# Attention, GLU and routed experts on one core: side work handed out twice per pair, squares moved to VectorE, the first experts' table a chunk earlier

## The chip, the cores and the metric

The kernel runs on one core of a Trainium2 chip. The metric is the device time of one execution in microseconds (us), taken over several runs. The engines are TensorE (PE; its weight loads are listed as PEld), VectorE (DVE), ScalarE (ACT), GpSimd (POOL) and SyncE (SP, which only issues DMAs here). Each engine works through its own instructions in the order in which they were written and stops at the first one whose inputs are not there.

## The reference, cut to what matters

```python
attn = np.maximum(z @ z.T / S, 0.0) ** 2            # 8 batches, S = 3072, z has 64 columns
x = u * (attn @ v)                                  # 24576 tokens of 256
xn = x / np.sqrt(np.mean(x * x, -1) + 1e-6) * rms_g
g = xn @ w_gate                                     # 256 -> 1536
x = (g * sigmoid(g) * (xn @ w_val)) @ w_out         # 1536 -> 256
e_idx = np.argmax(x @ r_gate, 1)                    # one of 8 experts for each token
for e in range(8):
    ye = np.maximum(x[e_idx == e] @ w1[e], 0.0) @ w2[e]      # 256 -> 1024 -> 256
    out[e_idx == e] = softmax_weight * sigmoid(x @ r_og)[e] * ye
```

Every product is made in float32 accuracy from pairs of a high and a low part, so most of them are three matmuls (high by high, high by low, low by high).

## The kernel before, in words

**Chunks and pairs.** The 24576 tokens are 48 chunks of 512 (six to a batch). For attention a chunk has 12 steps, one for each 256 keys (`Attn`, step n is chunk n // 12); for the GLU it has 12 steps, one for each 128 of the 1536 columns (`Glu`, step m). `pair(n, m)` writes one attention step and one GLU step side by side, with m = n - 18: first 18 attention steps stand alone, then come 558 pairs, then 6 GLU steps alone, and the 12 GLU steps of the last chunk. After these the experts run: 100 slots of 256 gathered tokens, four steps each (`Expert`).

**One pair on the engines.** TensorE gets the scores `s` of step n (L504, L505), the GLU products `g` of step m (L648), then the second halves of the steps before: attention times values into `o` (L535 to L537, `Attn.second`), and the GLU's output `y` (L673 to L675). ScalarE makes relu and square of the scores in `r` (L507, L512) and their high part `ha` (L515), the sigmoid `sg` (L652) and the high part `hg` (L660). VectorE makes the low parts `la` (L521) and `lg` (L663) and multiplies the gate (L656). The scores' tile `r` has two buffers, and four PSUM banks (`sc`) are shared by `s`, `g` and the small products of the side work.

**Side work.** All that a chunk needs between its attention and its GLU, and between its GLU and the experts, is cut into pieces that the class `Side` holds in two streams and a list of loaded jobs. Once in each pair, behind `a.high(0)`, `side.tick` hands out pieces until the pair's budget (4.0 for a pair, 1.5 for attention alone, 1.9 for the GLU alone, all in estimated us) is spent; stream 0 goes first. A piece that is only a time (no function) holds its stream until so much of the planned time has passed (7.94 for a pair, 3.75 and 4.19 for a step alone). `side.after(k, fn)` runs a function k ticks later. `side.until(...)` writes pieces out at once, without regard to a budget, until a condition holds.

**From attention to GLU.** When the last step of a chunk's attention is done, `Attn.leave` multiplies by `u` into `x` (L546, VectorE) and puts into stream 0: a time of 1.0, the squares (L552, four ACTIVATEs with a sum on ScalarE), 3.0, the root (L558 to L564, VectorE and GpSimd), 6.0, the scaling of `x` (L568, ScalarE), 2.0, and 16 block transposes into `xf` (L599 through `turn_x`, VectorE, named `turn_blocks` in the code). This chunk's GLU starts six pairs after its attention has ended. In the last pair ahead of it `until(g.J + 1 in turned)` writes what is left of the transposes, and `split_x` makes `xTh` (L628, ScalarE) and `xTl` (L629, VectorE), which the first `g` of the chunk reads.

**Weights at the start.** The GLU's weights come as 36 blocks of doubles and are decoded by `from_double`: two instructions on VectorE (L333, L334) and a square on ScalarE (L331), then `lower` (three on VectorE, L338 to L340, one on GpSimd, L341), then `parts` (high part on ScalarE, L93, low part on GpSimd, L96). `lower` comes one tick after the first part and `parts` two ticks after that. Two scratch buffers alternate; a decode that finds its buffer's previous decode unfinished writes the rest of that one out first (`chain.end()`). A GLU step m of the first chunk needs 3 (m + 1) decoded blocks and calls `until` for them.

**Experts.** `route` (stream 1) turns a finished chunk of `y` into expert numbers, gates and rows in DRAM (`xs`, `idl`), with 16 block transposes into `rec` (L615). `table(0)` (stream 1) makes the list of the first 12 slots (NSA) from the chunks that are routed by then: it counts, gathers list entries, transposes them on TensorE (`ids`, L894) and keeps them. It is started after GLU step m = 46 * 12, and behind step 3 of the last chunk's GLU `until(0 in tabs)` writes out what is left of it; then `begin_experts` loads weights and rows of slots 0 and 1 and starts the row transposes of slot 0 (`turn_rows`, L599 into `gTf`, which takes one of the two buffers of `sg`).

Of the kernel before, what the change touches and what calls it, by code (L numbers as in the profile page):

```python
# [19 lines left out]
LAG = 3  # L20
# [5 lines left out]
def attention_glu_routed(ctx: ExitStack, tc: tile.TileContext, u, v, z, w_gate, w_val, w_out, rms_g, r_gate, r_og, w1, w2, out):  # L26
# [31 lines left out]
    NSA = max(0, min(12, -((E * 255 - (NT - 1024)) // 256)))  # L58
# [429 lines left out]
    class Attn:  # L488
# [50 lines left out]
        def leave(self):  # L539
# [10 lines left out]
            def squares(k):  # L550
                for qb in (2 * k, 2 * k + 1):
                    nc.scalar.activation(out=uu[:, qb], in_=x[:, qb], func=AF.Square, accum_out=ss[:, qb : qb + 1])  # L552
                if k:
                    squared.add(J)
# [15 lines left out]
            side.add(1.0, None, 0)  # L570
            side.add(0.1, lambda: squares(0), 0)
            side.add(0.1, lambda: squares(1), 0)
            side.add(3.0, None, 0)
            side.add(0.4, root, 0)
            side.add(6.0, None, 0)
            side.add(0.1, lambda: scale(0), 0)
            side.add(0.1, lambda: scale(1), 0)
            side.add(2.0, None, 0)
# [363 lines left out]
    def known(stage):  # L942

        return NT if stage else (NJ - 2) * 512
# [114 lines left out]
    def begin_experts():  # L1059
        for s in range(2):  # L1060
            prepare(s)
            for part in range(4):
                load_weights(s, part)
        turn_rows(0)

    def spare(n):
        side.jobs(ej[:n])
        del ej[:n]
# [5 lines left out]
    last = {"a": None, "g": None}  # L1074
    lists = {}

    def pair(n, m):
# [11 lines left out]
        pa, pg = last["a"], last["g"]  # L1089
        last["a"], last["g"] = a, g  # L1090
        for step in (pa, pg):
            if step:
                step.second()
# [3 lines left out]
        t.time = (3.75 if a else 0.0) + (4.19 if g else 0.0)  # L1097
        t.budget = 4.0 if a and g else 1.5 if a else 1.9
# [15 lines left out]
        if pa and pa.kp == NP - 1:  # L1114
            pa.leave()
        if pg and pg.f == NF - 1 and pg.J < NJ - 1:
            pg.leave()
        if a:
# [13 lines left out]
            if a.J >= 2 and a.kp in (NP // 2, NP - 1):  # L1132
                spare(1)

    with tc.manual_schedule():
# [7 lines left out]
        for n in range(tail + AHEAD):  # L1143
            m = n - AHEAD
            if m == 0:
                side.until(lambda: 0 in turned, 0)
                split_x(0)
            pair(n if n < NJ * NP else None, m if m >= 0 else None)
            if m == (NJ - 2) * NF and NSA:

                table(0, lambda: s1)
# [7 lines left out]
        for f in range(NF):  # L1159
            pair(None, tail + f)  # L1160
            if f == LAG and NSA:
                side.until(lambda: 0 in tabs, 1)
                begin_experts()
# [68 lines left out]
```

## Time and profile before

| what | value |
|---|---|
| median of 3 runs | 6101.07 us (6096.69 to 6106.18) |
| profiled execution, its own time | 6110.35 us |
| its span, first to last instruction | 6108.6 us |
| PE, PEld, DVE, ACT, POOL busy | 96%, 84%, 68%, 56%, 19% |
| mean granted TensorE clock | 0.983 |
| matmuls | 35032 |

The span has these stretches: attention alone from 5.7 us (the first scores) to 124.3 us, pairs from there to 4766.6 us, the last six pairs and the GLU alone to 4928.6 us (the first expert matmul), experts to 6092 us. A row with a window says how long each engine was busy in it and how many instructions it ran; PEclk is the mean of the granted clock, where 1.00 is 2.4 GHz and 0.50 is 1.2 GHz.

### The profile page before, as it was taken

The page shows a single profiled execution, that of the slowest core. Times are in us where ns is not written, and L with a number is a line of the kernel's source. Part 1 is how long each engine was busy: PE and PEld are TensorE (multiplying, and loading weights), DVE is VectorE, ACT ScalarE, POOL GpSimd, SP SyncE. Part 2 cuts the span into 40 slices and gives each one's busy share as a digit, 9 for nine tenths or more (in the row PEclk, how much of TensorE's full clock was granted, in tenths as well). Part 3 has the DMA queues.
Part 4 walks back from the last instruction along what each step waited for, and adds up shares of the span by engine and source line. Part 5 has one row for each costly group of instructions (what it writes and reads, how often), then busy time and mean ns, then how long its engine had stood idle before and what let it go on. Part 6 is the DMA issues. An engine that isn't in the chain of part 4 may idle for free. (4 is left out here: it accounts for less than half of the span.)

```text
span 6108.6 us, 95345 instructions
## 1 busy us (share of the span) xinstructions
PE 5868.4 (96%) x35032; PEld 5155.5 (84%) x35032; DVE 4141.2 (68%) x8920; ACT 3418.4 (56%) x6610; POOL 1151.3 (19%) x1729
## 2 busy tenths in 40 slices
PE   6899999999999999999999999999999889999998
PEld 5688888888888888888888888888888779999998
DVE  6666666665666566666666666657565678888886
ACT  4566666666666666666666666666666423333332
POOL 2212101210121012101211030103000023333333
PEclk8999999999999999999999999999999999999999
DMA  2101100110010001001110010001000112232241
GB/s 70 47 25 49 34 25 30 46 34 23 30 49 30 23 30 49 30 27 32 47 32 22 29 32 13 15 12 36 8 15 8 47 55 101 101 103 101 102 139 57
DMA packets 199592, 268.27 MB, mean 44 GB/s; under 512 B 46988, under 2 KB 176016, under 8 KB 190928
## 3 DMA queue, kind: packets, MB, share of 16 engines
q1 hardware_dynamic: 173664, 210.29, 10.7%
q0 software_dynamic: 25456, 51.83, 2.7%
q8 instruction: 278, 4.55, 0.3%
q14 instruction: 194, 1.59, 0.1%
HBM read 528.71 MB, written 86.71 MB: 101 GB/s over the span
## 5 line engine op out<-in xcount | busy, mean ns | idle before, releaser
L537 PE MATMUL o<-v,la 128*128 128x256 f32 x4608 | 1298.3, 282 | 29.3 <-DVE la L521 29.2
L535 PE MATMUL o<-v,ha 128*128 128x256 f32 x4608 | 1291.9, 280 | 5.3 <-DVE ha L517 5.2
L536 PE MATMUL o<-v,ha 128*128 128x256 f32 x4608 | 1291.2, 280 | 0.0
L521 DVE TENSOR_TENSOR la<-r,ha 128x512 fp32r<-128x512 f32 x1152 | 835.9, 726 | 663.5 <-ACT ha L515 658.0
L507 ACT ACTIVATE r<-s 128x512 f32<-128x512 f32 x1152 | 624.8, 593 | 859.4 <-PE s L505 806.5
L648 PE MATMUL g<-xTh,wg 128*128 128x512 f32 x2304 | 844.7, 408 | 131.9 <-ACT xTh L628 102.7
L656 DVE TENSOR_TENSOR sg<-g,sg 128x512 f32<-128x512 f32 x1152 | 793.9, 689 | 196.0 <-ACT sg L652 133.5
L537 PEld LDWEIGHTS o<-v,la 128*128 128x128 f32 x4608 | 871.5, 189 | 33.2 <-DVE la L521 32.9
L535 PEld LDWEIGHTS o<-v,ha 128*128 128x128 f32 x4608 | 872.6, 189 | 29.5 <-DVE ha L517 6.4
L536 PEld LDWEIGHTS o<-v,ha 128*128 128x128 f32 x4608 | 871.9, 189 | 25.6
L648 PE MATMUL g<-xTh,wv 128*128 128x512 f32 x2304 | 831.2, 402 | 5.7 <-ACT wv L93 3.0
L515 ACT ACTIVATE ha<-r 128x512 fp32r<-128x512 f32 x1116 | 705.7, 632 | 38.6
L512 ACT ACTIVATE r<-r 128x512 f32<-128x512 f32 x1152 | 721.7, 627 | 1.0
L648 PEld LDWEIGHTS g<-xTh,wg 128*128 128x128 f32 x2304 | 443.2, 192 | 263.7 <-ACT xTh L628 122.9
L1007 PE MATMUL h<-gh,W 128*128 128x256 f32 x3200 | 641.2, 283 | 5.4 <-ACT gh L93 4.1
L660 ACT ACTIVATE hg<-sg 128x512 fp32r<-128x512 f32 x576 | 363.6, 631 | 487.2 <-DVE sg L656 431.3
L1026 PE MATMUL eo<-W,hx 128*128 128x512 f32 x1600 | 580.2, 395 | 0.7 <-DVE o L1039 0.7
L1007 PEld LDWEIGHTS h<-gh,W 128*128 128x128 f32 x3200 | 526.9, 191 | 25.3 <-ACT gh L93 5.5
L648 PEld LDWEIGHTS g<-xTh,wv 128*128 128x128 f32 x2304 | 446.1, 194 | 109.9 <-PE g L648 3.8
L599 DVE STREAM_TRANSPOSE gTf<-xg 32x128 f32<-32x128 f32 x1600 | 483.3, 302 | 49.2 <-DMA xg<-xs,clip 26.9
L1010 ACT ACTIVATE hx<-h 128x512 fp32r<-128x512 f32 x400 | 236.7, 595 | 496.0 <-PE h L1007 493.5
L96 POOL TENSOR_TENSOR le<-e_raw,he 128x512 fp32r<-128x512 f32 x64 | 83.0, 1297 | 2119.9 <-ACT he L93 2119.9
(170 smaller groups left out, 11046.8 us busy)
## 6 DMA issues: line engine op xcount, KB each, us to landing
W<-ws SPq DMA_DIRECT2D x400, 1024.0 KB
v_raw<-in_v SPq DMA_DIRECT2D x96, 256.0 KB
u<-in_u SPq DMA_DIRECT2D x48, 512.0 KB
xs<-rec SPq DMA_DIRECT2D x48, 512.0 KB
e_raw<-in_moe_w SPq DMA_DIRECT2D x64, 256.0 KB
ws<-he SPq DMA_DIRECT2D x64, 256.0 KB
ws<-le SPq DMA_DIRECT2D x64, 256.0 KB
z_raw<-in_z SPq DMA_DIRECT2D x48, 128.0 KB
```

The lines of the kernel that those rows point to most:

```text
L507: nc.scalar.activation(out=r, in_=ps, func=AF.Relu, scale=SCALE)
L512: nc.scalar.activation(out=r, in_=r, func=AF.Square)
L515: nc.scalar.activation(out=self.ab[j][0], in_=r, func=AF.Copy)
L521: nc.vector.tensor_tensor(out=l, in0=self.r[j], in1=h.bitcast(F32), op=ALU.subtract)
L535: nc.tensor.matmul(o, lhsT=ah[:, cs], rhs=vh, start=kb == 0 and qb % 2 == 0, stop=False, skip_group_check=True)
L536: nc.tensor.matmul(o, lhsT=ah[:, cs], rhs=vl, start=False, stop=False, skip_group_check=True)
L537: nc.tensor.matmul(o, lhsT=al[:, cs], rhs=vh, start=False, stop=kb == NK - 1, skip_group_check=True)
L599: nc.vector.transpose(out=ov[32 * q : 32 * q + 32, :, :, i, :], in_=iv[32 * i : 32 * i + 32, :, :, q, :])
L648: nc.tensor.matmul(ps, lhsT=a[:, d, fs], rhs=x[:, d], start=n == 0, stop=n == 5)
L656: nc.vector.tensor_tensor(out=self.sg, in0=ps, in1=self.sg, op=ALU.mult)
L1007: nc.tensor.matmul(o, lhsT=w[:, c0 : c0 + 128], rhs=x[:, d], start=n == 0, stop=n == 5)
L1026: nc.tensor.matmul(self.accs[t], lhsT=h[:, cs], rhs=w, start=f == 0, stop=False)
```

## The change

Five things are changed.

- `pair` calls `side.tick` twice, at the old place and at its end, each time with half of the time and half of the budget. `after(k)` therefore counts half pairs, and times such as 3.0 pass within one half pair (3.97).
- In stream 0 the squares come first, right behind the product with `u`, as four `scalar_tensor_tensor` with a sum on VectorE; the root follows at once, and the times are 3.0 and 1.0 where they were 1.0, 3.0, 6.0 and 2.0.
- While attention runs alone, `Attn.second` is written two steps late where it was one; the first pair with a GLU step writes two of them.
- `table(0)` starts after m = 45 * 12 and knows 45 chunks (NSA stays 12), `begin_experts` comes behind step 1 of the last chunk's GLU where it was step 3, and a time of 8.0 stands ahead of the row transposes of slot 0.
- `Attn.leave` is called for each step written.

```diff
-                    nc.scalar.activation(out=uu[:, qb], in_=x[:, qb], func=AF.Square, accum_out=ss[:, qb : qb + 1])
+                    nc.vector.scalar_tensor_tensor(
+                        out=uu[:, qb], in0=x[:, qb], scalar=1.0, in1=x[:, qb], op0=ALU.mult, op1=ALU.mult, accum_out=ss[:, qb : qb + 1]
+                    )
...
-            side.add(1.0, None, 0)
-            side.add(0.1, lambda: squares(0), 0)
-            side.add(0.1, lambda: squares(1), 0)
+            side.add(0.9, lambda: squares(0), 0)
+            side.add(0.9, lambda: squares(1), 0)
+            side.add(0.4, root, 0)
             side.add(3.0, None, 0)
-            side.add(0.4, root, 0)
-            side.add(6.0, None, 0)
             side.add(0.1, lambda: scale(0), 0)
             side.add(0.1, lambda: scale(1), 0)
-            side.add(2.0, None, 0)
+            side.add(1.0, None, 0)
             turn_x(J)
...
-        return NT if stage else (NJ - 2) * 512
+        return NT if stage else (NJ - 3) * 512
...
                 load_weights(s, part)
+        side.add(8.0, None, 0)
         turn_rows(0)
...
-        pa, pg = last["a"], last["g"]
-        last["a"], last["g"] = a, g
-        for step in (pa, pg):
+        pg, last["g"] = last["g"], g
+        if a:
+            last["a"].append(a)
+
+        gone = []
+        while len(last["a"]) > (1 if g and a else 2 if a else 0):
+            gone.append(last["a"].pop(0))
+        for step in (*gone, pg):
             if step:
                 step.second()
...
-        t.time = (3.75 if a else 0.0) + (4.19 if g else 0.0)
-        t.budget = 4.0 if a and g else 1.5 if a else 1.9
+
+        t.time = ((3.75 if a else 0.0) + (4.19 if g else 0.0)) / 2
+        t.budget = 2.0 if a and g else 0.75 if a else 0.95
         side.tick(t)
...
+        side.tick(t)
...
-            if m == (NJ - 2) * NF and NSA:
+            if m == (NJ - 3) * NF and NSA:
...
-            if f == LAG and NSA:
+            if f == 1 and NSA:
```

Where the instructions now stand is shown at three places.

**VectorE ahead of a chunk's GLU** (here chunk 27; `xf` holds the transposed chunk, `xTl` is the low part that `split_x` makes, `la`, `sg` and `lg` belong to the steps of the pairs). Before:

```order
L599 STREAM_TRANSPOSE xf<-x 32x4x2x32 x12
L521 TENSOR_TENSOR la<-r,ha 128x512
L656 TENSOR_TENSOR sg<-g,sg 128x512 x2
L599 STREAM_TRANSPOSE xf<-x 32x4x2x32 x4
L629 SCALAR_TENSOR_TENSOR xTl<-xf,g_p,xTh 128x512 x2
L521 TENSOR_TENSOR la<-r,ha 128x512
L663 TENSOR_TENSOR lg<-sg,hg 128x512
```

After:

```order
L599 STREAM_TRANSPOSE xf<-x 32x4x2x32
L521 TENSOR_TENSOR la<-r,ha 128x512
L656 TENSOR_TENSOR sg<-g,sg 128x512 x2
L521 TENSOR_TENSOR la<-r,ha 128x512
L663 TENSOR_TENSOR lg<-sg,hg 128x512
L521 TENSOR_TENSOR la<-r,ha 128x512
L656 TENSOR_TENSOR sg<-g,sg 128x512 x2
L629 SCALAR_TENSOR_TENSOR xTl<-xf,g_p,xTh 128x512 x2
L521 TENSOR_TENSOR la<-r,ha 128x512
```

Before, all 16 transposes stand in the pair of the split, four of them between the gate's product and `xTl`; now the last of them stands a whole pair earlier, and the others (6 and 9 in a row) in the two pairs before that.

**VectorE in the first chunk's GLU, ahead of the matmuls of its step 9** (`d` is the scratch of a weight decode, `w_raw` the block of doubles, `ss` and `yi` belong to a root). Before:

```order
L663 TENSOR_TENSOR lg<-sg,hg 128x512
L338 SCALAR_TENSOR_TENSOR d<-d 128x256
L339 TENSOR_SCALAR d<-d 128x256
L340 SCALAR_TENSOR_TENSOR d<-w_raw,d 128x256
L338 SCALAR_TENSOR_TENSOR d<-d 128x256
L339 TENSOR_SCALAR d<-d 128x256
L340 SCALAR_TENSOR_TENSOR d<-w_raw,d 128x256
L558 TENSOR_SCALAR ss<-ss 128x4
L559 TENSOR_SCALAR yi<-ss 128x4
```

After, the last two of three decodes that stand there one behind the other:

```order
L333 TENSOR_SCALAR d<-w_raw 128x256
L334 SCALAR_TENSOR_TENSOR d<-w_raw,d 128x256
L338 SCALAR_TENSOR_TENSOR d<-d 128x256
L339 TENSOR_SCALAR d<-d 128x256
L340 SCALAR_TENSOR_TENSOR d<-w_raw,d 128x256
L333 TENSOR_SCALAR d<-w_raw 128x256
L334 SCALAR_TENSOR_TENSOR d<-w_raw,d 128x256
L338 SCALAR_TENSOR_TENSOR d<-d 128x256
L339 TENSOR_SCALAR d<-d 128x256
L340 SCALAR_TENSOR_TENSOR d<-w_raw,d 128x256
L599 STREAM_TRANSPOSE xf<-x 32x4x2x32 x5
```

Before, two decodes were begun earlier and only their second parts stood here; now three whole decodes do, written out by `until` because stream 0 holds the ticks of these pairs.

**TensorE around the transposes of the first table** (`ids`; `y` and `g` are the GLU, `s` the scores). Before:

```order
L674 MATMUL y<-lg,wo_98 128x512
L675 MATMUL y<-hg,wo_99 128x512
L894 MATMUL ids<-ident,plain 128x12 x4
L648 MATMUL g<-xTh,wg_94 128x512
L648 MATMUL g<-xTl,wg_94 128x512
L648 MATMUL g<-xTh,wg_95 128x512
```

After:

```order
L674 MATMUL y<-lg,wo_98 128x512
L675 MATMUL y<-hg,wo_99 128x512
L894 MATMUL ids<-ident,plain 128x12 x4
L504 MATMUL s<-p 128x512
L505 MATMUL s<-q,p 128x512
L504 MATMUL s<-p 128x512
L505 MATMUL s<-q,p 128x512
L648 MATMUL g<-xTh,wg_94 128x512
```

They move from the GLU alone (its step 4 follows) into a pair that still has attention, six pairs ahead of the end of attention.

## Rows read from the trace of the kernel before

**Rows 1.** Windows: us, then busy us (instructions) of PE, PEld, DVE, ACT, POOL; PEclk, DMA share, GB/s.

```profile
5.70:124.30 118.60, 83.53 (x489) 74.57 (x490) 79.72 (x160) 54.13 (x113) 38.20 (x55) 0.88 0.24 71
124.30:144.60 20.30, 9.17 (x42) 7.21 (x41) 15.49 (x35) 9.13 (x19) 2.89 (x4) 0.66 0.09 26
144.60:220.70 76.10, 61.42 (x325) 51.35 (x324) 53.97 (x112) 43.62 (x88) 22.57 (x31) 0.93 0.20 60
220.70:273.50 52.80, 38.40 (x186) 31.38 (x185) 40.77 (x86) 28.32 (x64) 17.00 (x32) 0.87 0.16 50
369.90:4766.60 4396.70, 4295.78 (x24770) 3725.84 (x24769) 2828.51 (x5587) 2808.46 (x5382) 628.35 (x1146) 0.99 0.10 29
4766.60:4928.60 162.00, 135.72 (x643) 111.06 (x642) 96.68 (x223) 60.96 (x117) 13.73 (x25) 0.92 0.16 61
4928.60:5060.00 131.40, 114.68 (x750) 102.81 (x749) 115.95 (x347) 33.33 (x70) 43.36 (x43) 0.95 0.14 42
5060.00:6092.00 1032.00, 1031.81 (x7276) 966.69 (x7275) 846.60 (x2248) 314.24 (x635) 369.88 (x358) 1.00 0.30 103
```

**Rows 2.** Waits of PE from 369.9 to 4766.6: us in total, times, longest.

```profile
PE g L648 <- ACT xTh L628: 79.4, 44, 3.5
PE g L648 <- DVE xTl L629: 11.3, 40, 0.3
```

**Rows 3.** Windows inside the pairs: one chunk of 12, and windows of 50 us.

```profile
2776.00:2873.70 97.70, 96.25 (x562) 83.88 (x561) 63.33 (x125) 63.33 (x121) 10.11 (x19) 1.00 0.09 28
350.00:400.00 50.00, 47.62 (x271) 41.29 (x270) 31.62 (x54) 31.62 (x58) 6.14 (x14) 0.97 0.14 43
550.00:600.00 50.00, 46.10 (x253) 38.94 (x253) 31.95 (x54) 31.92 (x60) 21.72 (x41) 0.93 0.25 77
```

**Rows 4.** Timeline at a chunk's start: start, us, engine, line, tiles, count, [idle before <-releaser].

```profile
2865.78 5.37 DVE L599 STREAM_TRANSPOSE xf<-x 32x256 f32<-32x256 f32 x12
...
2871.79 1.48 DVE L656 TENSOR_TENSOR sg<-g,sg 128x512 f32<-128x512 f32 x2
...
2873.28 1.79 DVE L599 STREAM_TRANSPOSE xf<-x 32x256 f32<-32x256 f32 x4
...
2875.17 1.34 ACT L628 ACTIVATE xTh<-xf,g_p 128x512 fp32r<-128x512 f32 x2 [5.93 <-DVE xf L599]
...
2875.94 0.49 PE L648 MATMUL g<-xTh,wg 128*128 128x512 f32 x1 [1.16 <-ACT xTh L628]
```

**Rows 5.** Groups by shape: busy us, mean ns, idle before.

```profile
L552 ACT ACTIVATE u<-x 128x256 f32<-128x256 f32 x192 | 76.9, 402 | 0.0
L552 ACT ACTIVATION_READ_ACCUMULATOR u<-x 128x1 f32 x192 | 35.9, 187 | 0.0
L338 DVE SCALAR_TENSOR_TENSOR d<-d 128x256 f32<-128x256 f32 x36 | 15.1, 419 | 0.0
L341 POOL TENSOR_TENSOR d<-d 128x256 f32<-128x256 f32 x36 | 27.4, 761 | 132.9 <-DVE d L340 131.4 <-DVE ss L558 1.5
```

**Rows 6.** Waits at the end of the pairs and in the first experts, 4766.6 to 5060, of PE.

```profile
PE g L648 <- ACT xTh L628: 12.2, 2, 11.0
PE ids L894 <- DVE plain L888: 9.3, 1, 9.3
PE eo L1027 <- DVE lx L1013: 7.8, 5, 3.3
PE y L673 <- ACT hg L660: 4.4, 1, 4.4
```

**Rows 7.** Timeline ahead of the last chunk's GLU.

```profile
4847.94 7.17 DVE L599 STREAM_TRANSPOSE xf<-x 32x256 f32<-32x256 f32 x16
```

**Rows 8.** Waits of all engines from 0 to 320.

```profile
PE o L537 <- DVE la L521: 29.2, 15, 4.8
...
PE g L648 <- DVE sg L656: 25.6, 10, 6.8
...
DVE d L333 <- POOL wv L96: 13.5, 7, 3.4
...
DVE d L333 <- POOL wo L96: 11.8, 6, 2.9
DVE d L333 <- POOL wg L96: 11.6, 7, 2.2
...
PE g L648 <- ACT xTh L628: 11.1, 1, 11.1
```

## What the prediction says

> **What bounds the kernel now.** I read the windows first, to see in which stretch TensorE is idle or slow; then who it waits for there; then the timeline of one such wait; and last the groups by shape, for prices.
>
> [rows 1] split the span. From 5060 on TensorE is busy 1031.81 of 1032 us at clock 1.00: the change leaves that work as it is, and nothing is to be had there. From 369.9 to 4766.6 (44 chunks) it is busy 4295.78 of 4396.70 us: 100.9 us idle, and a clock of 0.99. The start (5.7 to 273.5) and the end of the pairs (4766.6 to 5060) are worse: 192.5 of 267.8 and 250.4 of 293.4 us busy, at clocks from 0.66 to 0.95.
>
> [rows 2] say where the 100.9 us go: 79.4 + 11.3 = 90.7 us are waits for `xTh` and `xTl`, once in nearly every chunk. [rows 4] show one. VectorE does 12 transposes in the last pair ahead of the chunk (5.37 us, so 0.448 each), then the gate's product, then the four that are left (1.79 us); ScalarE starts `xTh` only behind them, and the first `g` of the chunk waits 1.16 us. Elsewhere in the pairs VectorE and ScalarE are 64% busy and TensorE doesn't wait: a chunk is 96.25 us of matmuls in 97.70 [rows 3], some 8.0 us a pair. So the pairs are bound by TensorE, and what can be gained in them are the chunk starts and what the clock does behind them.
>
> **The clock.** In [rows 3] two windows show 0.97 and 0.93; of the 88 windows of 50 us in this stretch some two dozen are of that kind, each behind a wait for `xTh`, and the windows without a wait show 1.00, as the experts do for 1032 us. Half clock for a time costs half of that time, so a mean of c over W us costs (1 - c) W: 0.01 x 4396.7 = 44 us.
>
> **Part 1: half ticks and a shorter stream 0.** Before, with a tick of 7.94, the four times of stream 0 cost a tick each, and the transposes began in the last tick. Now squares and root go out in the half tick behind the product, 3.0 and 1.0 pass in one half tick each, and the 16 transposes (7.2 at 2.0 a half tick) are all out a pair or more ahead of `split_x`; the order of VectorE ahead of chunk 27 shows it. `xTh` then stands behind the sigmoid alone and has the time in which TensorE does `o`, `y` and the next `s`. I take the 90.7 us and the 44 us as gone: **-135**. The other 10 us of waits there stay. Bounds: -150 if these go too, -100 if a third of waits and dips stays.
>
> What hides the pieces: VectorE's largest lump is now nine transposes, 9 x 0.448 = 4.0 us, or squares, root and leave. Before it was 5.37 us in the same place [rows 4], and TensorE waited for nothing but `xTh`. If that cover were gone, TensorE would wait for a PSUM bank (first rival).
>
> **Part 2: squares on VectorE.** ScalarE loses 192 x (402 + 187) ns = 113 us [rows 5], beside other work; VectorE gets 192 instructions. The nearest row is `scalar_tensor_tensor` at 128 x 256, 419 ns; with a separate read of the sum as on ScalarE it would be 606. So 80 to 116 us, at most 2.4 in a chunk of 98 in which VectorE is idle for 34 [rows 3]: nothing on the path, 0. GpSimd runs 1/7 of the stretch [rows 1], and neither wait in [rows 2] is put down to it. The Trainium skill (SBUF — State Buffer, Who interferes with whom) says that a VectorE instruction with two SBUF inputs shuts out a GpSimd instruction that reads SBUF while it runs, which speaks against these squares. By that rule the squares of chunks 0 and 1, which fall among the weight decodes, would add up to 2 x 2.4 = 4.8 us to part 4; no row here shows such a wait, and the sum goes without it.
>
> **Part 3: the end of the pairs.** [rows 6] hold the terms.
> - The last chunk's `xTh`: 11.0 us, behind 16 transposes in one piece, 7.17 us [rows 7]. The halved ticks of the six GLU steps alone (0.95 each) leave four forced and two in the tick before: ten fewer, 4.5 us, and the scaling is no longer forced ahead of the sigmoid, some 1.5 us. -6.
> - The first table's transposes `ids`: 9.3 us, because the gather and what follows were forced out at once. They now stand among pairs and their pieces are spread over ticks. -9.3.
> - `y` behind `hg`, 4.4 us: VectorE stood waiting for the gathered rows ahead of the gate's product. The time of 8.0 puts the row transposes later. But `gTf` now holds one of the two `sg` buffers from step 1 to step 5 of that GLU, and nine transposes a step go with the gate's chain, so some wait can come back. -3.
> - `lx`, longest 3.3 us: `until` forces the route of chunk 46 in the fourth expert step, 16 transposes and more; now two pieces are left there. -3.3.
> - The clock: (1 - 0.92) x 162 = 13 us, of which I leave 3.4 for the wait that stays, -9.6; and -1.7 of 0.05 x 131.4 = 6.6 in the first experts.
>
> Sum **-33**; bounds -42 (nothing stays but the 5 us of `xTh`) and -20 (the `sg` buffer gives back the third and half of the clock).
>
> **Part 4: the start.** Here signs differ.
> - Attention alone, 118.6 us for 18 steps. TensorE waits 29.2 us for `la` [rows 8], but it isn't what holds the pace: `relu` needs one of two `r` tiles, which `la` frees. Writing `second` two steps late therefore moves TensorE's wait rather than ending it, and I count 0 for it. What slows VectorE are decodes whose buffer is still in use: 13.5 + 11.8 + 11.6 = 36.9 us over 20 decodes [rows 8], 1.8 each. With half ticks `parts` comes a pair and a half behind the first part, and the buffers are free by then. About seven decodes lie here, so -13 with the pieces that now go behind `la` and not ahead of it (bounds -30 and 0).
> - The wait of 11.1 us for the first `xTh` [rows 8] stays: the transposes are still forced there.
> - Pairs 18 to 24 keep two decodes a pair: -5 (bounds -15 and +5).
> - Pairs 25 to 29 get worse. Stream 0 now takes the ticks, so the steps 8 to 11 of the first chunk's GLU find seven decodes not begun, which `until` writes out in a row ahead of their matmuls (the order of VectorE shows two of three). One is five instructions of about 0.42 on VectorE and two of about 0.76 on GpSimd [rows 5], 3.6 us one behind the other. Before, the last 52.8 us [rows 1] held five pairs where 8.0 each would be 40: 12.8 us for three pairs with forced halves. I take 8 us more; the bounds are 0, if VectorE overlaps them with TensorE's `o` and `y`, and 7 x 3.6 = 25.
>
> Sum **-10**; bounds -45 and +30, in practice -35 and +20.
>
> **The sum.** The profiled execution took 6110.35 us: 6110.35 - 135 - 33 - 10 = 5932. The median of the runs is 9.3 us under the profiled one, so I say **5922**.
>
> **Rivals.**
> - *Slower: the pieces at the end of a pair stop TensorE's banks.* The tick behind `lg` and the next one ahead of the gate's product stand back to back on VectorE. If together they run past the time that it has between `lg` and the next product, `g` of the next pair finds no bank, in each of the six pairs of a chunk that have pieces. It decides from more than the 5.4 us that the trace already holds there without such a wait [rows 4]; to end slower it has to cost 178 us, 4 us in each of 44 chunks. Against it: 9 x 0.448 = 4.0, and a chunk in which VectorE is idle for a third. Priced at 4.5 us a chunk: 6101 + 20 = about 6120. Chance 3%.
> - *Half of the chunk start stays.* `xTh` and `xTl` have one buffer, so ScalarE can't write them before the old chunk's last `g` has read it, and square and `ha` stand behind it. If half of part 1 stays, 5922 + 68 = 5990. For it: xTl's 0.3 us are there in 40 chunks [rows 2]. Against it: in [rows 4] `xTh` waits 5.93 us for `xf`, not for `g`. Chance 8%.
> - *The forced decodes cost their full price* (+25 and their dips, with no gain in attention alone): 5922 + 8 to 45, about 5960. Chance 12%.
> - *The pairs have room that busy time hides.* TensorE's weight loads fill 3725.84 of 4396.70 us in the pairs, 84.7%, and 93.7% in the experts [rows 1]. If the pairs came up to the experts' share, they would take 4396.7 x 84.7 / 93.7 = 3974 us, and the kernel about 5630. The Trainium skill (Perfetto Trace Analysis, Identifying the Most-Contended Engine) has that share, not matmul busy time, as the measure of TensorE's headroom. Against it: more of the pairs' matmuls have 512 columns and so one weight load for twice the columns; nothing in the change shortens a matmul. Chance 2%.
>
> **How the numbers follow.** The forecast has 75%, with a range of its own from 5880 (start and end at their better bounds) to 5965. The range for 8 in 10 leaves out the first and last rivals and the far half of the second: **5875 to 5980**. What a measurement here can tell is about 0.2%, 12 us. All cases but the first end far below 6089: faster 0.95, same 0.02, slower 0.03.
>
> **What would show it.** In the profile after, waits of `g` for `xTh` between the second chunk and the last should be near none, and the windows of 50 us there should be busy all the time at clock 1.00; a chunk should take 96 to 96.5 us (99 where a batch begins). `ids` should have no wait, and the last `xTh` one of about 5 us. The start up to the second chunk's GLU (273.5 before) should be within 240 to 295, with the longest waits of `g` in pairs 26 to 29. I am wrong if chunks still take 98 or more, or if waits of `g` for `sg` show up all over the pairs.

## The result, and the profile after

The changed kernel takes 5902.14 us (median of 4 runs, 5901.62 to 5902.39), the kernel before beside it 6099.25 us (4 runs, 6096.69 to 6106.18): a ratio of 0.9675, with a 95% interval from 0.9658 to 0.9692. The forecast was 5922 with a range from 5875 to 5980. The span fell from 6108.6 to 5900.5 us with as many matmuls as before, and the mean granted clock rose from 0.983 to 0.992. The profile's busy line of the kernel after:

```profile
PE 5787.5 (98%) x35032; PEld 5122.6 (87%) x35032; DVE 4235.5 (72%) x9304; ACT 3345.8 (57%) x6226; POOL 1173.4 (20%) x1729
```

Windows of the kernel after (us, then busy us and instructions of PE, PEld, DVE, ACT, POOL; PEclk, DMA share, GB/s): attention alone, pairs 18 to 29, the 44 chunks, the end of the pairs, the first experts, and one chunk of 12 pairs. They answer to [rows 1, 3].

```profile
5.80:103.90 98.10, 73.47 (x464) 64.11 (x465) 77.40 (x157) 48.98 (x98) 37.15 (x52) 0.91 0.26 80
103.90:265.70 161.80, 115.09 (x572) 93.31 (x571) 126.73 (x256) 85.35 (x173) 46.94 (x70) 0.83 0.17 51
361.50:4588.00 4226.50, 4224.86 (x24770) 3704.55 (x24768) 2911.87 (x5971) 2743.03 (x5030) 649.77 (x1148) 1.00 0.10 30
4588.00:4727.00 139.00, 131.65 (x648) 108.12 (x647) 93.80 (x210) 56.44 (x104) 13.74 (x24) 0.98 0.18 69
4727.00:4850.00 123.00, 111.91 (x741) 100.53 (x740) 110.33 (x324) 33.25 (x70) 41.15 (x41) 0.97 0.16 47
2667.60:2763.30 95.70, 95.70 (x563) 83.99 (x562) 64.70 (x133) 61.92 (x113) 10.06 (x19) 1.00 0.09 28
```

Cut at the same events (the first scores; pair 18; pair 30; the last six pairs; the first expert matmul), the two spans differ so:

| stretch | before, us | after, us | difference | forecast |
|---|---|---|---|---|
| attention alone, 18 steps | 118.6 | 98.1 | -20.5 | |
| pairs 18 to 29 | 149.2 | 161.8 | +12.6 | -10 with the row above |
| pairs 30 to 41 | 96.4 | 95.7 | -0.7 | |
| 44 chunks | 4396.7 | 4226.5 | -170.2 | -135 |
| end of the pairs, GLU alone | 162.0 | 139.0 | -23.0 | |
| experts to the last matmul | 1163.8 | 1157.4 | -6.4 | -33 with the row above |

Four fifths of the gain lie in the 44 chunks. TensorE is idle there for 1.6 us in all (4226.50 less 4224.86), where it was 100.9, and the half clock is gone. The waits of PE from 361.5 to 4588 us in the kernel after (us in total, times, longest) are this one row, beside [rows 2]:

```profile
PE g L648 <- ACT r L507: 1.6, 7, 0.2
```

### The profile page after: what moved, and what is told of

It reads as the page before. It is cut to its first block, busy times and chain, and to the rows that moved or that the text cites. A ratio compares the mean times of both kernels' runs of the same rounds, so it can differ in the third digit from the quotient of the medians.

```text
span 5900.5 us, 95207 instructions
## 1 busy us (share of the span) xinstructions
PE 5787.5 (98%) x35032; PEld 5122.6 (87%) x35032; DVE 4235.5 (72%) x9304; ACT 3345.8 (57%) x6226; POOL 1173.4 (20%) x1729
## 5 line engine op out<-in xcount | busy, mean ns | idle before, releaser
L648 PE MATMUL g<-xTh,wg 128*128 128x512 f32 x2304 | 823.6, 398 | 49.0 <-ACT xTh L628 21.6
L648 PE MATMUL g<-xTh,wv 128*128 128x512 f32 x2304 | 817.4, 396 | 5.1 <-ACT wv L93 4.9
L778 POOL DMA_INDIRECT idl<-pair,ri x192 | 197.8, 1030 | 2121.1 <-DVE pair L765 1633.9
L648 PEld LDWEIGHTS g<-xTh,wg 128*128 128x128 f32 x2304 | 435.0, 189 | 160.5 <-ACT xTh L628 22.4
```

The source lines that it names most:

```text
L648: nc.tensor.matmul(ps, lhsT=a[:, d, fs], rhs=x[:, d], start=n == 0, stop=n == 5)
```

## What the experiments showed

Each experiment was run in rounds with the kernel before on the same chip. The runs e1 to e4, e5 to e8 and e9 to e11 shared one chip each, and e12 had another. The kernel before took 6113.62, 6111.66, 6114.60 and 6110.29 us (medians) beside them, and 6099.25 beside the kernel after; so the medians of the table come from different chips, and each ratio, with its 95% interval, is to the kernel before on the same chip. "Alone" is the 18 attention steps alone, "pairs" are pairs 18 to 29; the stretches are those of one profiled execution each.

| kernel | median, us | ratio | alone | pairs | 44 chunks | end |
|---|---|---|---|---|---|---|
| before | 6099.25 | 1 | 118.6 | 149.2 | 4396.7 | 162.0 |
| after | 5902.14 | 0.9675 [0.9658, 0.9692] | 98.1 | 161.8 | 4226.5 | 139.0 |
| e1_half_only | 5923.11 | 0.9688 [0.9672, 0.9704] | 104.4 | 152.1 | 4241.0 | 144.1 |
| e2_stream0_only | 5944.74 | 0.9722 [0.9706, 0.9738] | 117.0 | 152.3 | 4233.2 | 161.0 |
| e3_squares_act | 5912.17 | 0.9672 [0.9655, 0.9688] | 98.5 | 160.4 | 4234.0 | 140.1 |
| e4_lag1 | 5905.67 | 0.9659 [0.9643, 0.9675] | 102.0 | 157.1 | 4226.9 | 140.2 |
| e5_old_table | 5916.72 | 0.9687 [0.9671, 0.9703] | 97.7 | 160.8 | 4227.7 | 150.6 |
| e6_no8 | 5900.45 | 0.9659 [0.9642, 0.9675] | 97.9 | 161.7 | 4227.4 | 136.8 |
| e7_alone125 | 5904.50 | 0.9664 [0.9648, 0.9680] | 122.6 | 138.0 | 4227.0 | 138.9 |
| e8_all_early | 5912.05 | 0.9677 [0.9661, 0.9693] | 122.9 | 145.6 | 4227.0 | 138.9 |
| e9_ha_scalar | 5891.64 | 0.9637 [0.9621, 0.9653] | 87.1 | 160.8 | 4226.9 | 138.8 |
| e10_v_scalar | 5900.00 | 0.9649 [0.9633, 0.9665] | 93.8 | 161.7 | 4227.3 | 139.7 |
| e11_fill_sg | 5893.82 | 0.9639 [0.9623, 0.9655] | 90.0 | 160.5 | 4226.9 | 140.0 |
| e12_together | 5880.04 | 0.9623 [0.9610, 0.9636] | 78.1 | 159.9 | 4227.5 | 137.8 |

The intervals of the ratios are some 20 us wide, so small steps are read from the stretches. Where nothing was edited these repeat from kernel to kernel: the 44 chunks of e4 to e12 lie between 4226.9 and 4227.7, the other columns within 1.5 us. The experts, which are not in the table, spread by 3.8 us (1157.4 to 1161.2) among kernels with the same code for them.

### Which part clears the chunk starts: e1, e2 and e3

**e1** puts only the half ticks into the kernel before; squares and times stay as they were.

```diff
-        t.time = (3.75 if a else 0.0) + (4.19 if g else 0.0)
-        t.budget = 4.0 if a and g else 1.5 if a else 1.9
+        t.time = ((3.75 if a else 0.0) + (4.19 if g else 0.0)) / 2
+        t.budget = 2.0 if a and g else 0.75 if a else 0.95
...
+        side.tick(t)
```

> The kernel before with the two half ticks alone; squares, times of stream 0, lag and tables as before. Theory (TensorE loses at a chunk's start only because transposes are still to come there, and either part moves them clear of it): in the written order the last transpose stands a pair ahead of the split, so chunks take 95.7 to 96.3 us, waits of g for xTh between the chunks are near 0, and the time is 5905 to 5935. Rival (the gain needs the squares off ScalarE as well, or the shorter times): half of the 170 us stays, 5990 or more.

**e2** puts only the new stream 0 into the kernel before, with whole ticks.

```diff
-            side.add(1.0, None, 0)
-            side.add(0.1, lambda: squares(0), 0)
-            side.add(0.1, lambda: squares(1), 0)
-            side.add(3.0, None, 0)
+            side.add(0.9, lambda: squares(0), 0)
+            side.add(0.9, lambda: squares(1), 0)
...
-            side.add(6.0, None, 0)
+            side.add(3.0, None, 0)
...
-            side.add(2.0, None, 0)
+            side.add(1.0, None, 0)
```

with the four squares written as `nc.vector.scalar_tensor_tensor`, as in the kernel after.

> The kernel before with the new stream 0 alone (squares on VectorE at once, root, 3.0, 1.0), handed out in whole ticks; lag and tables as before. Theory as for e1_half_only: the transposes end a pair ahead of the split here too, so chunks take 95.7 to 96.3 us and the time is 5910 to 5945. Rival (finer pieces are what frees TensorE; lumps of nine transposes and ten route pieces in one tick bring other waits): chunks stay at 97 or more, 5980 or more.

The 44 chunks of e1 (columns as above):

```profile
358.00:4599.00 4241.00, 4230.13 (x24769) 3708.64 (x24768) 2831.10 (x5584) 2816.49 (x5382) 627.82 (x1147) 1.00 0.10 30
```

The same window of e2:

```profile
370.80:4604.00 4233.20, 4227.99 (x24769) 3704.87 (x24768) 2912.49 (x5937) 2740.23 (x5030) 627.98 (x1146) 1.00 0.10 30
```

Either part alone clears the chunk starts: 155.7 us are gone with e1 and 163.5 with e2, of 170.2 with both. Both times lie where the theory had them, and so do 37 of the 44 chunks (95.7 to 96.2 us). The gains don't add, since each part ends the same wait. The other seven chunks, in which the attention of a new batch begins, hold what is left; in e1 `g` waits there behind the scores' operand `p`:

```profile
PE g L648 <- DVE p L441: 9.2, 5, 2.0
```

What only the half ticks do is the start and the end: with e2 attention alone (117.0) and the end of the pairs (161.0) stand as before, and with e1 they fall to 104.4 and 144.1.

**e3** is the kernel after with the squares back on ScalarE, at the new place.

```diff
-                    nc.vector.scalar_tensor_tensor(
-                        out=uu[:, qb], in0=x[:, qb], scalar=1.0, in1=x[:, qb], op0=ALU.mult, op1=ALU.mult, accum_out=ss[:, qb : qb + 1]
-                    )
+                    nc.scalar.activation(out=uu[:, qb], in_=x[:, qb], func=AF.Square, accum_out=ss[:, qb : qb + 1])
```

> The changed kernel with the squares back on ScalarE, at their new place. Theory (both engines have idle time there, so the engine makes no difference): 5902 within 8 us, chunks 95.7 us. Rival (ScalarE's 2.4 us a chunk stand ahead of the next scores' relu and hold them up): 44 times 0.5 or more, 5925 or more.

Waits of PE in the 44 chunks of e3:

```profile
PE g L646 <- ACT r L507: 7.8, 14, 1.1
```

The squares of e3 by shape (busy us, mean ns | idle time of the engine before them, and what ended it):

```profile
L552 ACT ACTIVATE u<-x 128x256 f32<-128x256 f32 x192 | 77.6, 406 | 58.8 <-DVE x L546 58.7
```

The squares of the kernel after, with the read of their sum:

```profile
L552 DVE SCALAR_TENSOR_TENSOR u<-x 128x256 f32<-128x256 f32 x192 | 78.5, 464 | 0.0
L552 DVE DVE_READ_ACCUMULATOR u<-x 128x1 f32 x192 | 15.7, 82 | 0.0
```

By the ratio the two kernels can't be told apart. By the stretch the engine is worth 7.5 us (4234.0 against 4226.5). My theory, that the engine makes no difference, missed (5912.17, said 5902 within 8), and its rival's 5925 or more missed by far. At the new place, right behind the product, ScalarE has to stand and wait for `x` (58.7 us), and the relu behind it comes late for the next `g`. This tells only in the seven chunks in which the attention of a batch begins: they take 98.2 to 98.6 us, 97.2 to 97.5 in the kernel after, and the other 37 are alike. On VectorE the squares follow their own product, and 94.2 us of added work there make no wait of TensorE.

### The lag of attention alone: e4

```diff
-        while len(last["a"]) > (1 if g and a else 2 if a else 0):
+        while len(last["a"]) > (1 if a else 0):
```

> The changed kernel with attention alone one step late, as before. Theory (VectorE and the two tiles of r set the pace of attention alone; lag moves TensorE's wait and does not end it): attention alone 98 us within 4, 5902 within 8. Rival (the lag is what took attention alone from 118.6 to 98.1 us): 115 or more there, 5915 to 5925.

Windows of e4, attention alone and pairs 18 to 29:

```profile
5.90:107.90 102.00, 79.58 (x489) 69.92 (x490) 80.77 (x163) 52.91 (x106) 38.35 (x53) 0.92 0.28 85
107.90:265.00 157.10, 112.31 (x549) 90.24 (x548) 122.10 (x249) 81.47 (x164) 45.27 (x68) 0.87 0.16 47
```

Without the lag of two, attention alone takes 3.9 us more and the pairs behind it 4.7 less, as the theory had it. The instruction counts say why: TensorE does 489 matmuls ahead of pair 18 instead of 464, and 549 behind it instead of 572. The lag moves the second halves of one attention step over the border. It also lengthens the wait for the first `xTh`, here first in e4, then in the kernel after:

```profile
PE g L648 <- ACT xTh L628: 8.3, 1, 8.3
PE g L648 <- ACT xTh L628: 15.2, 1, 15.2
```

### The first experts' table: e5 and e6

**e5** takes the table's part back out of the kernel after.

```diff
-        return NT if stage else (NJ - 3) * 512
+        return NT if stage else (NJ - 2) * 512
...
-        side.add(8.0, None, 0)
...
-            if m == (NJ - 3) * NF and NSA:
+            if m == (NJ - 2) * NF and NSA:
...
-            if f == 1 and NSA:
+            if f == LAG and NSA:
```

with `NT - 1024` in the formula of NSA, as before.

> The changed kernel with the old table and experts' start (46 chunks known, table after m = 46 * 12, experts behind step 3, no time of 8.0). Theory (the table is worth what its forced wait and the route that is left over cost, and half ticks already took part of both): 139.0 + 1157.4 us from pair 570 on become 143 to 150 + 1158 to 1162, time 5906 to 5917. Rival (the whole of the 9.3 us of ids, the 4.4 of y and their clock come back): 20 us or more, 5922 or more.

Waits of PE from 4588 to 4750 us in e5:

```profile
PE g L648 <- ACT xTh L628: 6.6, 1, 6.6
PE ids L894 <- DVE plain L888: 3.8, 1, 3.8
PE y L673 <- ACT hg L660: 3.0, 1, 3.0
```

Waits of PE from 4588 to 4850 us in the kernel after, against [rows 6]:

```profile
PE g L648 <- ACT xTh L628: 6.4, 1, 6.4
PE h L1007 <- ACT gh L93: 6.2, 4, 1.8
PE eo L1027 <- DVE lx L1013: 1.9, 4, 0.6
...
PE y L673 <- ACT hg L660: 0.7, 1, 0.7
```

The gain at the end comes apart in part. All other edits together bring the stretch from 162.0 to 150.6 and the wait for `xTh` from 11.0 to 6.6; the earlier table brings it to 139.0, and the waits for `ids` and `y` (3.8 and 3.0 us here) go. The 11.6 us aren't a price of the table by itself: the half ticks alone (e1), with the old table, reach 144.1 and have no wait for `ids`. Why it comes up again beside the new stream 0 was not followed up. The experts take 3.0 us less with the earlier table, which is within their spread; the wait for `lx` in the first of them goes from 5.3 us to 1.9.

**e6** takes only the time of 8.0 ahead of the row transposes out of the kernel after.

```diff
-        side.add(8.0, None, 0)
```

> The changed kernel without the time of 8.0 ahead of slot 0's row transposes. Theory (VectorE then stops at the transposes until the gathered rows are there, ahead of the gate's product, as before the change): a wait of y or g of 2 to 5 us behind it, 5904 to 5910. Rival (two steps later the rows come no earlier than needed, the time is idle caution): 5902 within 3.

The end takes 136.8 us where it takes 139.0, and the wait for `xTh` of 6.4 us is then the only one there. The 8.0 costs 1 to 2 us of a stretch (137.8 in e12, also without it; 138.8 to 140.2 in the kernels that have it and the new table) and saves nothing. The rival was right, and my reason for the 8.0 (it keeps VectorE from standing ahead of the gate's product) has no support.

### The weights at the start: e7 and e8

**e7** gives attention alone a larger budget, so that the decodes which `until` forces in pairs 25 to 29 go out earlier; **e8** also gives the pairs of the first chunk 2.6.

```diff
-        t.budget = 2.0 if a and g else 0.75 if a else 0.95
+        t.budget = (2.0 if g.J == 0 else 2.0) if a and g else 1.25 if a else 0.95
```

```diff
-        t.budget = 2.0 if a and g else 0.75 if a else 0.95
+        t.budget = (2.6 if g.J == 0 else 2.0) if a and g else 1.25 if a else 0.95
```

> The changed kernel with a budget of 1.25 in each half tick of attention alone, where it is 0.75: 16 blocks of weights are decoded ahead of the first GLU step where it was 9, no decode is written out whole by until in steps 8 to 11, and 7 transposes of chunk 0 are forced where it was 13. Theory (the forced decodes and transposes are what pairs 18 to 29 lose against before): pairs 18 to 29 take 135 to 150 us (161.8), attention alone 98 to 108 (98.1), time 5885 to 5897. Rival (the decodes cost the same wherever they stand, VectorE's time sets both): attention alone up by as much as the pairs fall, 5902 within 5.

> As e7_alone125, and a budget of 2.6 in each half tick of the pairs with the first chunk's GLU: all 36 blocks are decoded by its step 8 and nothing is forced there. Theory: pairs 18 to 29 take 125 to 145 us, time 5878 to 5895. Rival (more pieces in a half tick hold up the gate's product, and TensorE waits for banks in pairs 18 to 25): pairs 18 to 29 at 150 or more, 5895 or more.

Windows of e7, attention alone and pairs 18 to 29:

```profile
5.60:128.30 122.70, 81.11 (x465) 69.98 (x465) 90.43 (x193) 54.40 (x114) 46.41 (x66) 0.86 0.27 81
128.30:266.20 137.90, 107.26 (x570) 89.46 (x571) 107.03 (x219) 78.95 (x156) 37.16 (x55) 0.89 0.15 44
```

Waits of PE in e7 from 5.8 to 262 us:

```profile
PE g L648 <- ACT xTh L628: 14.2, 1, 14.2
PE g L648 <- DVE sg L656: 11.0, 6, 4.1
```

Waits of PE at the start of e8, and the same row of the kernel after:

```profile
PE g L648 <- DVE sg L656: 22.0, 8, 4.1
PE g L648 <- DVE sg L656: 8.2, 4, 4.1
```

My theory, that decodes cost more where they are forced, fell. Seven blocks moved from the pairs into attention alone: alone grew by 24.5 us and the pairs shrank by 23.8. A decode costs about 3.5 us on either side, forced or not, so neither side has cover for it. Of the 24.5 us VectorE's own work is 13.0 (90.43 less 77.40), and its waits for a scratch buffer that GpSimd still reads, none in attention alone of the kernel after, are 8.1 in e7. e8 is worse than e7 by 7.6 us in the pairs: with more pieces in a tick, `g` waits twice as long for a bank that the gate's product on VectorE frees. That is the mechanism of the first rival; at the start it is there with budgets of 2.0 too, and was before the change (25.6 us [rows 8]).

The wait for the first `xTh` stands at 14.2 us in e7 with 7 forced transposes, and at 15.2 in the kernel after with 13. So the forced transposes aren't what sets most of it. The lag of two is worth 6.9 us of it (e4); no run took the rest of that chain apart.

### What bounds attention alone: e9, e10, e11 and e12

Three edits of the kernel after: **e9** makes the high part `ha` of attention alone on ScalarE, **e10** the high parts of the first batch's values, and **e11** takes the tile of fill values for the list `idl` from the buffers of `sg`, not of `r`.

```diff
-            a.high(0, nc.scalar if g else nc.vector)
+            a.high(0, nc.scalar)
...
-            a.high(1, nc.scalar if g else nc.vector)
+            a.high(1, nc.scalar)
```

```diff
-... (nc.gpsimd, nc.gpsimd) if b else (nc.vector, nc.gpsimd))
+... (nc.gpsimd, nc.gpsimd) if b else (nc.scalar, nc.gpsimd))
```

```diff
-        fill = f32t("r", "fill")
+        fill = f32t("sg", "fill")
```

> The changed kernel with the high part ha of attention alone on ScalarE, where it is on VectorE: 36 casts of 0.51 us leave VectorE. Theory (VectorE's work sets the pace of the start, which is why moving decodes about in e7_alone125 brought nothing): attention alone 98.1 falls to 85 to 93 us, pairs 18 to 29 stay at 162 within 5, time 5890 to 5897. Rival (the chain relu, square, ha, la with two tiles of r sets the pace, and ha takes longer on ScalarE): attention alone 98 to 108, 5900 to 5910.

> The changed kernel with the high parts of the first batch's values on ScalarE, where they are on VectorE: 24 casts of 0.55 us, all ahead of 45 us. Theory (as e9_ha_scalar, VectorE's work sets the pace): 5 to 10 us less up to attention step 6, 5892 to 5897. Rival (loads and GpSimd's low parts set it there): 5902 within 4.

> The changed kernel with the tile from which the lists are filled taken from the buffers of sg, where it is one of the two of r. Theory (relu waits 8.7 us for the fill's DMAs to have read it, TensorE 8.1 us behind it): that wait ends, start 5 to 9 us shorter, 5893 to 5898. Rival (VectorE has the decodes and the values' casts to do in that time anyway): the time goes to waits for la, 5900 within 4.

Window of e9, attention alone:

```profile
5.80:92.90 87.10, 72.38 (x464) 64.49 (x465) 62.68 (x126) 67.58 (x129) 35.44 (x52) 0.92 0.29 89
```

The 36 high parts of the kernel after as a group (from 0 to 130 us), and one of them in the timeline:

```profile
L517 DVE CAST ha<-r 128x512 fp32r<-128x512 f32 x36 | 25.7, 713 | 16.5 <-ACT r L512 15.8
```

```profile
84.40 0.75 POOL L341 TENSOR_TENSOR d<-d 128x256 f32<-128x256 f32 x1 [2.88 <-DVE d L340]
84.46 0.96 DVE L517 CAST ha<-r 128x512 fp32r<-128x512 f32 x1
```

In the kernel after VectorE is busy for 77.4 of the 98.1 us, more than any other engine. The 0.51 and 0.55 us of the two expectations are means of the kernel before. In the kernel after the 36 high parts take 0.71 us each (25.7), and with them off VectorE (e9) the stretch shrinks by 11.0 us. The 24 casts of the values take 0.42 each (10.1), and with them off (e10) it shrinks by 4.3. So work taken off VectorE shortens attention alone, though by less than half of its own time. For e9 the theory holds. e10's 5900.00 us lie within its rival's range and not its theory's: 0.7 us are gone at the scores of attention step 6 and 3.6 at those of step 7, where the theory had 5 to 10.

What made `ha` longer is GpSimd: 20 of the 36 started while a TENSOR_TENSOR of GpSimd ran, and each of these ended some 0.28 us behind it, as in the two rows (at 85.42 and 85.15). The other 16 took 0.41 to 0.43 us. In the kernel before six were held up so. With some 0.53 us each, the 20 are 10.6 us of VectorE's time; no run separates this from the rest of what e9 takes off.

e11 is another thing. The timeline of the kernel after at the fill's DMA and the relu that waits for it:

```profile
44.70 0.64 SPq L163 DMA_DIRECT2D idl<-fill  x1
...
48.66 0.60 ACT L507 ACTIVATE r<-s 128x512 f32<-128x512 f32 x1 [8.70 <-DMA idl<-fill]
```

The fill tile holds one of the two buffers of `r` until a DMA has read it, and the relu waits 8.7 us for that buffer. With another buffer the wait is gone and the stretch shrinks by 8.1 us.

**e12** is the kernel after with the edits of e9, e11 and e6.

> The changed kernel with three edits that each gave time or cost none: ha on ScalarE in attention alone (e9), the fill's tile from the buffers of sg (e11), no time of 8.0 (e6). Theory (the waits are apart: VectorE's casts all along attention alone, the fill once at 41 us, the experts' first rows at the end): the gains add, 11 + 8 + 2 us, attention alone near 80 us, time 5878 to 5885, ratio 0.9605 to 0.963. Rival (the step that waits for the fill hides VectorE's work of that time): the fill adds 3 or less, 5885 to 5892.

Window of e12, attention alone:

```profile
5.90:83.90 78.00, 69.34 (x464) 62.87 (x465) 62.65 (x126) 67.55 (x129) 35.68 (x52) 0.96 0.34 100
```

The gains add: 20.0 us in attention alone (11.0 and 8.1 apart) and 1.2 at the end, which is within the spread. At 5880.04 us, 0.9623 [0.9610, 0.9636] of the kernel before, it is the fastest of all here. What is left alone is 78.0 us with TensorE busy for 69.3.

## Why the prediction was right, and where it was off

Against the profiled execution of before the forecast was -178, and the spans differ by -208; the medians differ by -197, since that execution was 11 us above the median of before and the one after stands on its own median. The forecast had taken off 9.3 us for this, which is why it ends 20 us from the measured time and not 30. The 30 are 35 of part 1, less some 6 of parts 3 and 4.

**Part 1, the chunk starts: the mechanism was right, the term 35 us too small.** Said -135, bounded at -150; measured -170.2, outside the bound. The timeline of the kernel after at a chunk's start, against [rows 4]:

```profile
2758.98 1.48 DVE L656 TENSOR_TENSOR sg<-g,sg 128x512 f32<-128x512 f32 x2
...
2759.28 1.34 ACT L628 ACTIVATE xTh<-xf,g_p 128x512 fp32r<-128x512 f32 x2 [0.46 <-PE g L648]
...
2760.38 1.41 DVE L629 SCALAR_TENSOR_TENSOR xTl<-xf,g_p,xTh 128x512 fp32r<-128x512 f32 x2
...
2764.20 0.40 PE L648 MATMUL g<-xTh,wg 128*128 128x512 f32 x1
2764.44 0.40 PE L648 MATMUL g<-xTl,wg 128*128 128x512 f32 x1
```

No transpose stands at the split any more. `xTh` now waits only for the old chunk's last `g` (0.46 us), is done at 2760.62 (2759.28 and 1.34), and TensorE wants it at 2764.20, 3.6 us later.

The size went wrong in how I priced the wait. I added up the listed idle times, and these run from the modelled end of the matmul before. The timeline of the kernel before, first the last scores and then the second and third products of the chunk (the first, at 2875.94, is in [rows 4]):

```profile
2873.94 0.39 PE L505 MATMUL s<-q,p 128*128 128x512 f32 x1
...
2874.17 0.39 PE L504 MATMUL s<-p 128*128 128x512 f32 x1
...
2874.39 0.39 PE L505 MATMUL s<-q,p 128*128 128x512 f32 x1
...
2876.73 0.50 PE L648 MATMUL g<-xTl,wg 128*128 128x512 f32 x1 [0.29 <-DVE xTl L629]
2877.07 0.62 PE L648 MATMUL g<-xTh,wg 128*128 128x512 f32 x2
```

From 2874.39 to 2877.07 there are three steps from one matmul to the next, which without a wait take 0.23 us each (2873.94 to 2874.17): 0.69. They took 2.68, so 1.99 us were lost, while 1.16 and 0.29, 1.45 in all, are listed. A chunk says the same: 97.70 us before [rows 3] and, in 30 of the 44 chunks, 95.73 after, 1.97 less, at clock 1.00 both times. So 0.54 us stood in no row of waits, some 24 us if all 44 chunk starts are like this one. The "other 10 us of waits" that I left in place went down to 1.6: 8.6 more. The clock gave 46 for my 44 (92.2 us at half clock before, none after; 5.4 of them fell into listed waits, so it may be 43). Together 90.7 + 24 + 8.6 + 46 = 169 of 170.2.

**Part 2, squares on VectorE at nothing: right.** An instruction and its sum take 464 and 82 ns in the mean, 94.2 us for 192 by the groups above, inside the 80 to 116. They aren't just harmless: at their new place, VectorE beats ScalarE by the 7.5 us of e3. The 464 is a mean of two kinds: 165 of the 192 ran beside no instruction of GpSimd and took 411 to 425 ns, as the nearest row (419) had it, and 23 of the other 27 took 573 to 982.

The rule on the shared read port had given 4.8 us for part 4. GpSimd's low parts of the experts' weights show such a thing in the 44 chunks of the kernel after, but not with the squares:

```profile
L96 POOL TENSOR_TENSOR le<-e_raw,he 128x512 fp32r<-128x512 f32 x62 | 91.9, 1482 | 1151.3 <-ACT he L93 1147.2 <-PE g L648 4.1
```

In e3, whose squares are on ScalarE:

```profile
L96 POOL TENSOR_TENSOR le<-e_raw,he 128x512 fp32r<-128x512 f32 x62 | 80.3, 1295 | 1178.7 <-ACT he L93 1178.7
```

In the kernel after 36 of the 62 take 1.29 to 1.30 us, as in e3, and 26 take 1.74 (the profile calls spans on GpSimd rough, but each size repeats within 0.01 us). None of the 62 overlaps a square. Each of the 26 starts 0.13 us behind `lg`, an instruction of VectorE with two inputs in SBUF. Where GpSimd starts first it is VectorE that is held up: `la`, mostly 0.69 us, takes 1.80 in 32 places. Two places in the timeline:

```profile
2730.82 0.72 DVE L663 TENSOR_TENSOR lg<-sg,hg 128x512 fp32r<-128x512 f32 x1 [0.15 <-ACT hg L660]
2730.96 1.74 POOL L96 TENSOR_TENSOR le<-e_raw,he 128x512 fp32r<-128x512 f32 x1
...
1719.11 1.30 POOL L96 TENSOR_TENSOR le<-e_raw,he 128x512 fp32r<-128x512 f32 x1 [4.53 <-ACT he L93]
1719.16 1.80 DVE L521 TENSOR_TENSOR la<-r,ha 128x512 fp32r<-128x512 f32 x1
```

This agrees with the Trainium skill (SBUF — State Buffer, Who interferes with whom): a VectorE instruction with two SBUF inputs contends with a GpSimd instruction that reads SBUF, and the order of issue decides which of the two is blocked. In the 44 chunks it costs nothing, since TensorE waits for 1.6 us in all. The prediction's "no row here shows such a wait" holds only for its own rows: the trace of before has 32 `la` of 1.80 us as well.

**Part 3, the end: right, but for the clock.** Said -33; measured -23.0 and -6.4, -29.4. The last `xTh` waits 6.4 us (said about 5), `ids` no more (0.2), `y` 0.7, and `lx` 0.6 at longest. In the end of the pairs TensorE's idle time fell by 18.9 us (26.3 to 7.4), where the terms for `xTh`, `ids` and `y` say 18.3. The clock's -9.6 was too large: of 27.3 us at half clock before, 13.9 fell into waits of TensorE, where there was no matmul to slow down. That leaves (27.3 - 13.9) / 2 = 6.7 us of loss where I had 13, and 2.1 after by the same sum (6.8 and 2.7): -4.6, and with the idle time -23.5 of the -23.0. What I feared of the `sg` buffer didn't come up; the wait of `h` for `gh` in the first experts rose from 4.1 to 6.2 us.

**Part 4, the start: the sum came out by luck.** Said -13 - 5 + 8 = -10; measured -20.5 in attention alone, +1.1 in pairs 18 to 24 and +11.6 in pairs 25 to 29 (87.3 and 61.9 us before, 88.4 and 73.4 after), -7.9 in all with rounding. All engines' waits from 0 to 320 us in the kernel after, against [rows 8]:

```profile
ACT r L507 <- DMA idl<-fill: 8.7, 1, 8.7
DVE d L333 <- POOL wg L96: 7.9, 5, 2.1
DVE d L333 <- POOL wv L96: 5.4, 3, 2.1
DVE d L333 <- POOL wo L96: 2.7, 2, 1.7
```

- The waits for a decode's buffer fell from 36.9 us over 20 to 16.0 over 10. But the argument for -13 put seven of them into attention alone: there the kernel before has 6.3 us over four, and the kernel after none. So they are at most 6 of the 20.5 us.
- The -20.5 is partly a shift, and what the rest comes from is shown only down to the half ticks. The kernel after begins 9 decodes ahead of the first GLU step where the kernel before began 11; at 3.5 us each (e7) that would be 7 us moved into the pairs, and the lag of two moves 3.9 more (e4). These 10.9 us, an estimate, are most of the pairs' +12.6. The lag, counted at 0 net, is 0 net. The half ticks alone (e1), with 11 decodes there and a lag of one, gain 14.2 us in attention alone and lose 2.9 in the pairs: -11.3, of which 3.4 are lost again with the other parts of the change.
- The "-5" in pairs 18 to 24 didn't come. The "+8" in pairs 25 to 29 priced the forced decodes by their being forced, and e7 shows that a decode costs about the same wherever it stands in this start. The +8 also rests on a wrong count: the last 52.8 us of before [rows 1] hold four pairs (26 to 29), not five, so the loss in them was 20.8 us and not 12.8. The longest waits of `g` for decoded weights do stand in pairs 27 to 29, as forecast.
- The first `xTh` wait, said to stay at 11.1, grew to 15.2, the longest wait of all; with a lag of one it is 8.3 (e4). The lag was counted as if it touched attention alone.

**The rivals.** None came about. Bank waits are absent from the 44 chunks; at the start they are there, and longer with a larger budget (e8). Nothing of the chunk start stayed. The forced decodes cost less than their full price of 25, and attention alone gained. The weight loads fill 3704.55 of 4226.50 us, 87.7%, while TensorE is busy for all but 1.6: the share rose because the idle time went. Whether there is room behind it no run shows; nothing here shortened a chunk below 95.73 us. That is also less than the 96 to 96.5 said, and the chunks in which a batch begins take 97.2 to 97.5, said 99.

## What to carry to other kernels

Side work that is cut fine and handed out often lets a bounded engine run without gaps, and it is enough that the last piece is done one step ahead of its reader: here either finer ticks or an earlier stream alone did nearly all of it. Price a gap by the time from one issue to the next against an undisturbed place, not by the idle time listed, which can understate it. And look at a stretch's neighbours before crediting a change: two of the edits at the start (the lag of two, and e7's earlier decodes) only moved work over a border, while one tile that shared a buffer name with the busiest chain cost 8 us. And look at what a mean is made of before giving it a cause: the 26 slow low parts of GpSimd ran beside another instruction than the one that had been moved.

## What the hardware showed that I had not expected

- Waits listed per matmul add up to less than the time lost: 1.45 against 1.99 us at a chunk's start.
- The half clock of [rows 3] went with waits of 1.2 to 3.5 us. With these gone, the granted clock was 1.00 in every part of 4226 us, without any change to the matmuls: 46 of the 170 us.
- A sum along the free axis cost VectorE 82 ns to read beside 464 ns of work (419 with no GpSimd instruction beside it); on ScalarE the same pair is 402 and 187 [rows 5].
- An instruction of VectorE that starts while a TENSOR_TENSOR of GpSimd runs can be held until that one is over: 0.42 us becomes 0.96 (`ha`), 0.69 becomes 1.80 (`la`). The other way about, 1.30 became 1.74 (`le`).
